# Reordered loads, a held channel product, grouped value products and merged output stores in an attention and mixer kernel

## The chip, the cores and the metric

The kernel runs on one core of one Trainium2 chip. The metric is the device time of one execution in microseconds (us), lower is better. Times are medians of several executions; the profile is one execution, whose span is some 2 us shorter than the time of that same run.

## The reference

Attention with a squared ReLU in place of softmax, its result fed to an MLP mixer (first over tokens, then over channels):

```python
# q, k, v: (8, 12, 448, 64)
scores = q @ k.T / sqrt(64)
attn   = maximum(scores, 0) ** 2 / 448
x      = (attn @ v), heads side by side         # (8, 448, 768)
h = maximum(x.T @ w_tok1, 0) @ w_tok2           # 448 -> 256 -> 448, over tokens
u = x + h.T
out = u + maximum(u @ w_ch1, 0) @ w_ch2         # 768 -> 1536 -> 768, over channels
```

Inputs and output are float32; the kernel computes in bfloat16.

## The kernel before

The work goes in 24 steps of four heads (three steps are one batch). A step transposes q and k on TensorE, makes seven blocks of scores, applies ReLU on ScalarE and squares on VectorE, multiplies by v, transposes the result x back, and does the token products. The channel products of an earlier batch lie in a queue and fill TensorE between them. One unit of the first product is 6 matmuls (about 1.16 us), one of the second 12 (about 1.96 us).

```python
def load_four(i):                       # q, k, v of step i, two transfers each
    ...
        first = i == 0 and name != "v"  # step 0: float32 on SyncE's and ScalarE's queues
        eng = (nc.sync if name == "q" else nc.scalar) if first else nc.gpsimd
        ...
            if first: ...               # and a cast
XDMA = 6                                # up to here x goes back by TensorE, then by DMA
def x_back(i):
    if i >= XDMA:
        for r in range(2):
            nc.sync.dma_start_transpose(out=x_sb[:, r], in_=xT[b % 2][:, 2 * d + r, :])
        return
    ...
def channel2(b, t, half):               # after 12 matmuls and an add into o, [128, 768]
    ...
    if half == 1:
        for k in range(2):              # two stores of 64 rows
            bb, c = divmod(2 * t + k, QC)
            nc.sync.dma_start(
                out=out[2 * (b // 2) + bb].rearrange("(p c) m -> c p m", c=QC)[c],
                in_=o[64 * k : 64 * (k + 1), :],
            )
def channel_work(b):                    # 12 units of the first product, then the second
    ...
# start: loads 0, 1, wt1, 2, wt2, 3, both halves of wc1; then 4, wc2/0, 5, wc2/1, ...
for i in range(DB + 1, ND + 2):         # the steps from 4 on
    scores(i, 0); scores(i, 1)
    values(i - 1, range(5))
    scores(i, 2)
    values(i - 1, range(5, QC)); values_out(i - 1); x_back(i - 1)
    ... fill(1/3) ... scores, transposes(i + 1), token1, token2, fill ...
```

Of the kernel before, what the change touches and what calls it, by code (L numbers as in the profile page):

```python
# [9 lines left out]
FP32 = mybir.dt.float32  # L10
# [6 lines left out]
def kernel(  # L17
# [11 lines left out]
    nc = tc.nc  # L29

    B, H, S, D = q.shape
    DM = H * D
# [5 lines left out]
    DB = H // 4  # L38
    QC = S // 64
    CC = DM // 128  # L40
    EC = DC // 128
# [27 lines left out]


    raws = {}
    first32 = {n: consts.tile([128, 2, QC, D], FP32, name=f"{n}_first") for n in ("q", "k")}

    def load_four(i):
        b, d = divmod(i, DB)
        tiles = []
        for name, src in (("q", q), ("k", k), ("v", v)):
            t = raw.tile([128, 2, QC, D], BF16, name=f"{name}_raw")
            first = i == 0 and name != "v"
            dst = first32[name] if first else t  # L80
            eng = (nc.sync if name == "q" else nc.scalar) if first else nc.gpsimd
            for r in range(2):
                h0 = 4 * d + 2 * r
                eng.dma_start(  # L84
                    out=dst[64 * r : 64 * (r + 1)].rearrange("p g c d -> p g (c d)"),
                    in_=src[b, h0 : h0 + 2].rearrange("g (p c) d -> p g (c d)", c=QC),
                )
            if first:
                if name == "q":
                    nc.vector.tensor_copy(t, dst)  # L90
                else:
                    nc.scalar.copy(t, dst)
            tiles.append(t)
        raws[i] = tiles

# [18 lines left out]
    def load_wc1(i, parts):  # L114
        n = DC // parts
        nc.gpsimd.dma_start(
            out=wc1[:, :, i * n : (i + 1) * n],
            in_=moe_w_ch1.rearrange("(g p) n -> p g n", p=128)[:, :, i * n : (i + 1) * n],
        )
# [11 lines left out]
    def transposes(i, early=False):  # L131
        sb = attn.tile([128, 2, 2, S], BF16, name="qkT")
        if not early:
            both = ps_acc.tile([128, 2, 1024], BF16, tag="acc", name="qkT_ps")
        parts = []
        for w in range(2):
            src = raws[i][w]
            ps = ps_mm.tile([128, 1024], BF16, tag="bank", name="qkT_ps1") if early else both[:, w]
            for c in range(QC):
                for g in range(2):  # L140
                    nc.tensor.matmul(  # L141
                        ps[64 * g : 64 * (g + 1), c * 128 : (c + 1) * 128],
                        lhsT=src[:, g, c, :],
                        rhs=ident,
                        is_transpose=True,
                        start=True,
                        stop=True,
                        skip_group_check=True,
                    )
            parts.append(ps)  # L150
        for w in range(2):
            copy = nc.scalar.copy if early and w == 0 else nc.vector.tensor_copy
            copy(  # L153
                sb[:, :, w, :].rearrange("n r (c p) -> n r c p", c=QC),
                parts[w][:, : 2 * S].rearrange("n (c r p) -> n r c p", c=QC, r=2),
            )
        qkT[i] = sb

    def scores(i, c):
# [54 lines left out]


    x_tiles, r1_tiles, uT_tiles = {}, {}, {}
    XDMA = 6

    def x_back(i):
        b, d = divmod(i, DB)  # L220
        x_sb = mix.tile([128, 2, 4, 128], BF16, name="x_sb")
        x_tiles[i] = x_sb
        if i >= XDMA:
            for r in range(2):
                nc.sync.dma_start_transpose(
                    out=x_sb[:, r], in_=xT[b % 2][:, 2 * d + r, :]
                )
            return
        for r in range(2):
            ps = ps_mm.tile([128, 1024], BF16, tag="bank", name="x_ps")  # L230
            for c in range(4):
                nc.tensor.matmul(
                    ps[:, c * 128 : (c + 1) * 128],
                    lhsT=xT[b % 2][:, 2 * d + r, c * 128 : (c + 1) * 128],
                    rhs=ident,
                    is_transpose=True,
                    start=(c == 0),
                    stop=(c == 3),
                )
            (nc.scalar.copy if r == 0 else nc.vector.tensor_copy)(  # L240
                x_sb[:, r], ps[:, :512].rearrange("n (c d) -> n c d", c=4)
            )

# [76 lines left out]
    def channel2(b, t, half):  # L320
        r2 = r2_tiles[b // 2]
        cols = slice(half * HN, (half + 1) * HN)
        if half == 0:
            out_tiles[b, t] = outp.tile([128, DM], FP32, name="out_sb")
        o = out_tiles[b, t]
        ps = ps_mm.tile([128, 512], FP32, tag="bank", name="m2_ps")
        for e in range(EC):
            nc.tensor.matmul(  # L328
                ps[:, :HN],
                lhsT=r2[:, e, t * 128 : (t + 1) * 128],  # L330
                rhs=wc2[:, e, cols],
                start=(e == 0),
                stop=(e == EC - 1),
            )
        nc.vector.tensor_tensor(  # L335
            out=o[:, cols].rearrange("n (g d) -> n g d", d=128),
            in0=ps[:, :HN].rearrange("n (g d) -> n g d", d=128),
            in1=u_tiles[b][:, half * (CC // 2) : (half + 1) * (CC // 2), t - chunks(b).start, :],
            op=ALU.add,
        )  # L340
        if half == 1:
            for k in range(2):
                bb, c = divmod(2 * t + k, QC)
                nc.sync.dma_start(
                    out=out[2 * (b // 2) + bb].rearrange("(p c) m -> c p m", c=QC)[c],
                    in_=o[64 * k : 64 * (k + 1), :],
                )
            out_tiles.pop((b, t))

    queue = []  # L350
    C1 = 6 * 189
    C2 = 12 * 163

    def channel_work(b):
        u_back(b)
        for e in range(EC):
            queue.append((C1, lambda e=e: channel1(b, e)))
        for t in chunks(b):
            for j in range(2):
                queue.append((C2, lambda t=t, j=j: channel2(b, t, j)))  # L360

    RESERVE = 2500.0
    credit = [-RESERVE]
    per_step = (EC * C1 + NT * C2) / DB

    def fill(share):
        if not queue:
            return
        credit[0] += share * per_step
        while queue and credit[0] > 0:  # L370
            cost, unit = queue.pop(0)
            credit[0] -= cost
            unit()


    PRE = 2
    gate = consts.tile([1, 1], BF16, name="gate")
    warm = consts.tile([128, 512], BF16, name="warm")
    nc.vector.memset(warm, 0.0)
# [12 lines left out]
    load_wt2()  # L392
    load_four(3)
    load_wc1(0, 2)
    load_wc1(1, 2)


    transposes(0, early=True)
    for i in range(DB + 1):
        for c in range(QC):  # L400
            scores(i, c)
            square(keep=1)
            if c < 3 and i > 0:
                values(i - 1, (4 + c,))
                if c == 2:
                    values_out(i - 1)
            if i < DB:
                if c == 3:
                    transposes(i + 1, early=True)
                if c == 4 and i > 0:  # L410
                    x_back(i - 1)
                if c == 5:
                    values(i, (0, 1))
                if c == 6:
                    if i > 0:
                        token1(i - 1)
                    values(i, (2, 3))
                if c == 0 and i > 1:
                    token2(i - 2, early=True)
                if c == 6 and i == 1:  # L420
                    order_wt2()
            else:
                if c == 0:
                    token2(i - 2, early=True)
                if c == 3:
                    x_back(i - 1)
                if c == 4:
                    transposes(i + 1)
                    token1(i - 1)
                if c == 6:  # L430
                    token2(i - 1)
                    channel_work(0)
        if i == 1:
            load_four(4)
            load_wc2(0, 4)
        if i == 2:
            load_four(5)
            load_wc2(1, 4)
    square()
    fill(1 / 3)  # L440

    for i in range(DB + 1, ND + 2):
        if i < ND:
            scores(i, 0)
            scores(i, 1)
        if 0 <= i - 1 < ND:
            values(i - 1, range(5))
        if i < ND:
            scores(i, 2)
        if 0 <= i - 1 < ND:  # L450
            values(i - 1, range(5, QC))
            values_out(i - 1)
            x_back(i - 1)
        if i + PRE < ND:
            if i - 1 >= XDMA:
# [57 lines left out]
```

## Time and profile before

| | before |
|---|---|
| time, median | 403.9 us (403.4 to 404.1) |
| span of the profile | 403.3 us |
| TensorE busy | 380.2 us (94%) |
| TensorE idle, first 100 us | 16.5 us |
| TensorE idle, 100 to 350 us | 1.2 us |
| after the last add | 4.1 us |

The first row is what counts. The prediction below shows and reads the lines behind the others.

### The profile page before, as it was taken

What the parts mean: (1) busy time and instruction counts of PE and PEld (TensorE: products, weight loads), DVE (VectorE), ACT (ScalarE), POOL (GpSimd) and SP (SyncE); (2) the same over time, 40 slices, a digit from 0 to 9 for tenths busy, and PEclk for the clock granted to TensorE, in tenths of its full rate; (3) what the DMA queues carried; (4) which work ended last, traced back from release to release, by engine and by line L of the source; (5) the groups of instructions that cost most, each with busy time, mean ns of one, the idle gap of its engine ahead of it and who ended that gap; (6) DMA issues with size and microseconds to landing.
All of it is one profiled execution on the core that took longest, in us unless ns stands there. A gap on an engine that the chain in (4) does not pass through costs nothing.

```text
span 403.3 us, 8721 instructions
## 1 busy us (share of the span) xinstructions
PE 380.2 (94%) x3609; PEld 205.0 (51%) x3609; DVE 205.5 (51%) x376; ACT 215.9 (54%) x302; POOL 95.8 (24%) x175
## 2 busy tenths in 40 slices
PE   5777888989999999999999999999999999999995
PEld 2344354555545645555445555555445555455563
DVE  1688453465445654565435755456525655452021
ACT  2899367445764456645664456644673456621400
POOL 7952553000123203303033123113033030000000
PEclk9999699999999999999999999999999999999999
DMA  8999999014456596358556496168555592125223
GB/s 172 131 196 202 196 167 167 13 41 106 81 80 119 106 176 91 50 98 164 102 70 121 100 184 98 33 105 153 125 71 88 118 167 61 28 50 117 58 55 102
DMA packets 71880, 43.97 MB, mean 109 GB/s; under 512 B 46048, under 2 KB 68256, under 8 KB 71840
## 3 DMA queue, kind: packets, MB, share of 16 engines
q0 software_dynamic: 24160, 21.24, 37.3%
q1 hardware_dynamic: 47392, 21.71, 25.7%
q10 hardware_dynamic: 288, 0.46, 0.5%
q8 instruction: 28, 0.46, 0.5%
q14 instruction: 12, 0.10, 0.1%
HBM read 43.38 MB, written 11.01 MB: 135 GB/s over the span
## 4 chain that ended last, share of the span: by engine, by line
PE 85%; DMA 7%; DVE 3%; ACT 2%; issue 1%; SPq 1%; POOL 0%; ACTq 0%; DVEq 0%
PE m_ps L328 27%; PE m_ps L311 25%; PE sc_ps L165 10%; PE acc_ps L193 7%; PE t_ps L249 5%; PE qkT_ps L141 5%; PE h_ps L273 5%; DMA k_raw<-in_k_dram 4%; DMA q_first<-in_q_dram 2%; ACT at L174 1%; DVE uT_sb L281 1%; DMA x_sb<-xT 1%; DVE xT L207 1%; DVE at L181 1%; ACT x_sb L240 0%
## 5 line engine op out<-in xcount | busy, mean ns | idle before, releaser
L174 ACT ACTIVATE at<-sc_ps 128x896 bf16<-128x896 f32 x168 | 143.8, 921 | 61.1 <-PE sc_ps L165 61.1
L311 PE MATMUL m_ps<-uT_sb,wc 128*128 128x448 bf16 x576 | 117.6, 353 | 1.3 <-DVE uT_sb L281 0.9
L328 PE MATMUL m_ps<-wc,r_sb 128*128 128x384 bf16 x672 | 116.2, 326 | 0.2 <-ACT x_sb L240 0.2
L181 DVE TENSOR_TENSOR at<-at 128x896 bf16<-128x896 bf16 x168 | 97.1, 617 | 7.9 <-ACT at L174 7.9
L328 PEld LDWEIGHTS <-r_sb 128*128 128x128 bf16 x672 | 64.6, 98 | 44.5 <-issue 2.8
L318 ACT ACTIVATE r_sb<-m_ps 128x448 bf16<-128x448 f32 x96 | 52.2, 544 | 64.2 <-PE m_ps L311 64.2
L311 PEld LDWEIGHTS <-wc 128*128 128x128 bf16 x576 | 54.9, 98 | 55.3 <-issue 8.1
L335 DVE TENSOR_TENSOR out_sb<-m_ps,u_sb 128x384 f32<-128x384 f32 x56 | 31.0, 554 | 56.3 <-PE m_ps L328 56.3
L165 PE MATMUL sc_ps<-qkT 64*64 64x448 bf16 x672 | 53.6, 372 | 3.4 <-ACT at L174 2.5
L207 DVE TENSOR_SCALAR xT<-acc_ps 128x448 bf16<-128x448 f32 x48 | 27.7, 619 | 54.2 <-PE acc_ps L193 54.2
L456 POOL COPY gate<-x_sb 1x1 bf16<-1x1 bf16 x15 | 2.7, 177 | 194.7 <-DMA x_sb<-xT 194.7
L281 DVE TENSOR_TENSOR uT_sb<-h_ps,xT 128x448 bf16<-128x448 f32 x48 | 27.7, 619 | 33.7 <-PE h_ps L273 33.7
L153 DVE COPY qkT<-qkT_ps 128x896 bf16<-128x896 bf16 x44 | 25.6, 619 | 33.1 <-PE qkT_ps L141 33.1
L193 PE MATMUL acc_ps<-at,v_raw 64*64 64x448 bf16 x672 | 42.2, 350 | 0.0
L165 PEld LDWEIGHTS <-qkT 64*64 64x64 bf16 x672 | 17.0, 106 | 36.1 <-issue 31.6
L257 ACT ACTIVATE r_sb<-t_ps 128x512 bf16<-128x512 f32 x24 | 14.4, 600 | 34.0 <-PE t_ps L249 34.0
L84 POOL DMA_DIRECT2D v_raw<-in_v_dram x48 | 29.8, 648 | 8.2 <-PE acc_ps L193 4.4
L84 POOL DMA_DIRECT2D q_raw<-in_q_dram x46 | 27.7, 612 | 16.9 <-DMA wc<-in_moe_w_ch_dram 12.1
L84 POOL DMA_DIRECT2D k_raw<-in_k_dram x46 | 28.0, 631 | 1.4 <-DMA k_raw<-in_k_dram 1.0
L249 PE MATMUL t_ps<-x_sb,wt 128*128 128x256 bf16 x192 | 25.8, 279 | 1.4 <-DMA x_sb<-xT 0.7
L193 PEld LDWEIGHTS <-v_raw 64*64 64x64 bf16 x672 | 20.4, 107 | 10.1 <-issue 1.1
L273 PE MATMUL h_ps<-wt,r_sb 128*128 128x448 bf16 x96 | 23.0, 364 | 0.7 <-ACT wt L109 0.7
(32 smaller groups left out, 116.1 us busy)
## 6 DMA issues: line engine op xcount, KB each, us to landing
out_dram<-out_sb SPq DMA_DIRECT2D x56, 192.0 KB, 2.9
v_raw<-in_v_dram POOLq DMA_DIRECT2D x48, 112.0 KB, 5.1
q_raw<-in_q_dram POOLq DMA_DIRECT2D x46, 112.0 KB, 3.6
k_raw<-in_k_dram POOLq DMA_DIRECT2D x46, 112.0 KB, 4.4
wc<-in_moe_w_ch_dram POOLq DMA_DIRECT2D x2, 1152.0 KB, 13.5
wc<-in_moe_w_ch_dram POOLq DMA_DIRECT2D x4, 576.0 KB, 10.0
u_sb<-uT_sb SPq DMA_TRANSPOSE x48, 3.7
x_sb<-xT SPq DMA_TRANSPOSE x36, 2.4
```

The lines of the kernel that those rows point to most:

```text
L84: eng.dma_start(out=dst[64 * r : 64 * (r + 1)].rearrange("p g c d -> p g (c d)"), in_=src[b, h0 : h0 + 2].rearrange("g (p c) d -> p g (c d ...
L165: nc.tensor.matmul(ps[64 * r : 64 * (r + 1), g, :S], lhsT=sb[h, r, 1, c * 64 : (c + 1) * 64], rhs=sb[h, r, 0, :], start=True, stop=True, s ...
L174: nc.scalar.activation(at, ps[:, :, :S], AF.Relu)
L181: nc.vector.tensor_tensor(out=at, in0=at, in1=at, op=ALU.mult)
L193: nc.tensor.matmul(ps[64 * g : 64 * (g + 1), r, :S], lhsT=v_raw[h, g, c, :], rhs=at[h, g, :], start=(c == 0), stop=(c == QC - 1), skip_gro ...
L207: nc.vector.tensor_scalar(out=xT[b % 2][:, 2 * d + r, :S], in0=ps[:, r, :S], scalar1=float(alpha2), scalar2=None, op0=ALU.mult,)
L249: nc.tensor.matmul(ps[:, j, :], lhsT=wt1[:, c, j * 128 : (j + 1) * 128], rhs=x_sb[:, :, c, :], start=(c == 0), stop=(c == 3),)
L273: nc.tensor.matmul(parts[r][:, :S], lhsT=r1[:, j, r * 128 : (r + 1) * 128], rhs=wt2[:, j, :], start=(j == 0), stop=(j == JC - 1),)
L281: nc.vector.tensor_tensor(out=uT_tiles[b // 2][:, 2 * d + r, off : off + S], in0=parts[r][:, :S], in1=xT[b % 2][:, 2 * d + r, :S], op=ALU.add,
L311: nc.tensor.matmul(ps[:, :S], lhsT=wc1[:, g, e * 128 : (e + 1) * 128], rhs=uT[:, g, off : off + S], start=(g == 0), stop=(g == CC - 1),)
L318: nc.scalar.activation(r2[:, e, off : off + S], ps[:, :S], AF.Relu)
L328: nc.tensor.matmul(ps[:, :HN], lhsT=r2[:, e, t * 128 : (t + 1) * 128], rhs=wc2[:, e, cols], start=(e == 0), stop=(e == EC - 1),)
```

## The change

Its intent is to bring each load when it is needed: the first q and k go first in GpSimd's queue and are cast on the way, the second half of the first channel weight comes after the next q, k, v, and the second channel weight a step later. The second channel product of the first batch is therefore held until the second batch. The value products stand together ahead of the third score block. The output stores change too: where both 64-row groups of a tile belong to one batch, they go out as one store of 2 x 64 rows.

```diff
-    first32 = {...float32 tiles of the first q and k...}
-            first = i == 0 and name != "v"
-            eng = (nc.sync if name == "q" else nc.scalar) if first else nc.gpsimd
-                eng.dma_start(
+                nc.gpsimd.dma_start(
...
-    XDMA = 6
+    XDMA = 7
...                                   # both copies of an x transpose on VectorE
-            (nc.scalar.copy if r == 0 else nc.vector.tensor_copy)(
+            nc.vector.tensor_copy(
...                                   # stores
-            for k in range(2):
-                bb, c = divmod(2 * t + k, QC)
-                nc.sync.dma_start(
-                    out=out[2 * (b // 2) + bb].rearrange("(p c) m -> c p m", c=QC)[c],
-                    in_=o[64 * k : 64 * (k + 1), :],
-                )
+            if b0 == b1:
+                nc.sync.dma_start(out=rows[b0][c0 : c0 + 2, :, part], in_=o[:, part])
+            else:
+                ...                   # two stores of 64 rows, as before
...                                   # the last tile is stored in two halves of its columns
-                queue.append((C2, ...channel2...))
+                later.append((C2, ...channel2...))
+        if b > 0:
+            queue.extend(later); later.clear()
+    rate = [EC * C1 / 3.5]            # back to the full rate from step 7 on
-    PRE = 2
+    PRE = 3
-    load_wc1(1, 2)                    # moved behind load_four(4); wc2 one step later
...
-            values(i - 1, range(5))
+            values(i - 1, range(QC))
+            values_out(i - 1)
             scores(i, 2)
-            values(i - 1, range(5, QC))
-            values_out(i - 1)
```

More of the change, by code (lines that the diff above doesn't have):

```diff
@@ L71 @@
     raws = {}
-    first32 = {n: consts.tile([128, 2, QC, D], FP32, name=f"{n}_first") for n in ("q", "k")}
     def load_four(i):
@@ L78, in load_four @@
             t = raw.tile([128, 2, QC, D], BF16, name=f"{name}_raw")
-            first = i == 0 and name != "v"
-            dst = first32[name] if first else t
-            eng = (nc.sync if name == "q" else nc.scalar) if first else nc.gpsimd
             for r in range(2):
                 h0 = 4 * d + 2 * r
-                eng.dma_start(
-                    out=dst[64 * r : 64 * (r + 1)].rearrange("p g c d -> p g (c d)"),
+                nc.gpsimd.dma_start(
+                    out=t[64 * r : 64 * (r + 1)].rearrange("p g c d -> p g (c d)"),
                     in_=src[b, h0 : h0 + 2].rearrange("g (p c) d -> p g (c d)", c=QC),
                 )
-            if first:
-                if name == "q":
-                    nc.vector.tensor_copy(t, dst)
-                else:
-                    nc.scalar.copy(t, dst)
             tiles.append(t)
@@ L134, in transposes, with copies @@
             both = ps_acc.tile([128, 2, 1024], BF16, tag="acc", name="qkT_ps")
+        def copies(w, ps):
+            halves = [slice(0, 2)] if i > 0 or w == 0 else [slice(0, 1), slice(1, 2)]
+            for n, r in enumerate(halves):
+                on_act = early and (w == 0) == (i > 0) and n == 0
+                (nc.scalar.copy if on_act else nc.vector.tensor_copy)(
+                    sb[:, r, w, :].rearrange("n r (c p) -> n r c p", c=QC),
+                    ps[:, : 2 * S].rearrange("n (c r p) -> n r c p", c=QC, r=2)[:, r],
+                )
         parts = []
@@ L150, in transposes @@
             parts.append(ps)
-        for w in range(2):
-            copy = nc.scalar.copy if early and w == 0 else nc.vector.tensor_copy
-            copy(
-                sb[:, :, w, :].rearrange("n r (c p) -> n r c p", c=QC),
-                parts[w][:, : 2 * S].rearrange("n (c r p) -> n r c p", c=QC, r=2),
-            )
+            if early:
+                copies(w, ps)
+        if not early:
+            for w in range(2):
+                copies(w, parts[w])
         qkT[i] = sb
@@ L340, in channel2 @@
         )
-        if half == 1:
-            for k in range(2):
-                bb, c = divmod(2 * t + k, QC)
-                nc.sync.dma_start(
-                    out=out[2 * (b // 2) + bb].rearrange("(p c) m -> c p m", c=QC)[c],
-                    in_=o[64 * k : 64 * (k + 1), :],
-                )
+        last = b == B - 1 and t == NT - 1
+        if half == 1 or last:
+            part = cols if last else slice(0, DM)
+            (b0, c0), (b1, c1) = divmod(2 * t, QC), divmod(2 * t + 1, QC)
+            rows = [out[2 * (b // 2) + n].rearrange("(p c) m -> c p m", c=QC) for n in range(2)]
+            if b0 == b1:
+                nc.sync.dma_start(
+                    out=rows[b0][c0 : c0 + 2, :, part],
+                    in_=o[:, part],
+                )
+            else:
+                for k, (n, c) in enumerate(((b0, c0), (b1, c1))):
+                    nc.sync.dma_start(
+                        out=rows[n][c, :, part], in_=o[64 * k : 64 * (k + 1), part]
+                    )
+        if half == 1:
             out_tiles.pop((b, t))
-    queue = []
+    queue, later = [], []
     C1 = 6 * 189
@@ L359, in channel_work @@
             for j in range(2):
-                queue.append((C2, lambda t=t, j=j: channel2(b, t, j)))
-    RESERVE = 2500.0
-    credit = [-RESERVE]
-    per_step = (EC * C1 + NT * C2) / DB
+                later.append((C2, lambda t=t, j=j: channel2(b, t, j)))
+        if b > 0:
+            queue.extend(later)
+            later.clear()
+    credit = [0.0]
+    rate = [EC * C1 / 3.5]
     def fill(share):
@@ L368, in fill @@
             return
-        credit[0] += share * per_step
+        credit[0] += share * rate[0]
         while queue and credit[0] > 0:
@@ L434 @@
             load_four(4)
-            load_wc2(0, 4)
+            load_wc1(1, 2)
         if i == 2:
             load_four(5)
+            load_wc2(0, 4)
+        if i == 3:
+            load_four(6)
             load_wc2(1, 4)
     square()
-    fill(1 / 3)
+    fill(1 / 2)
     for i in range(DB + 1, ND + 2):
+        if i == 2 * DB + 1:
+            rate[0] = (EC * C1 + NT * C2) / DB
         if i < ND:
```

## The prediction

> **What bounds the kernel now.** I first read the strip of 40 slices on the page, then a table by windows, because the change acts at the start and the page's averages mix stages.
>
> ```profile
> PE   5777888989999999999999999999999999999995
> PEclk9999699999999999999999999999999999999999
> DMA  8999999014456596358556496168555592125223
> ```
>
> The reader is to see three stages: some 50 us in which TensorE is only 0.5 to 0.8 busy while the DMA engines are full and one slice (40 to 50 us) has a low clock; a long stage in which TensorE is full; and a short end. The window table gives sizes (columns: window, its length, busy us and instruction count of PE, PEld, DVE, ACT, POOL, then granted clock, DMA share, GB/s):
>
> ```profile
> 0.00:10.00 10.00, 5.51 (x37) 2.61 (x37) 1.45 (x5) 2.91 (x4) 7.36 (x18) 1.00 0.90 172
> 10.00:20.00 10.00, 7.77 (x102) 3.90 (x99) 5.96 (x10) 8.42 (x11) 9.74 (x17) 1.00 0.98 131
> 20.00:30.00 10.00, 7.79 (x128) 4.46 (x125) 8.74 (x17) 9.49 (x14) 5.26 (x8) 1.00 1.17 195
> 30.00:40.00 10.00, 7.78 (x118) 4.24 (x114) 8.98 (x18) 9.21 (x14) 2.41 (x4) 1.00 1.21 201
> 40.00:50.00 10.00, 8.00 (x76) 3.95 (x74) 4.50 (x8) 3.94 (x6) 5.62 (x10) 0.66 1.22 195
> ...
> 100.00:350.00 250.00, 248.81 (x2426) 134.16 (x2425) 136.42 (x249) 142.96 (x201) 56.08 (x105) 1.00 0.62 104
> ```
>
> From 100 to 350 us TensorE idles 250 - 248.8 = 1.2 us: nothing is to be had there by reordering, since the change removes no matmul. The idle time is in front: 4.5 us of the first ten, then 2.2, 2.2, 2.2 and 2.0. From 10 to 40 us ScalarE (8.4 to 9.5 of 10) with VectorE right behind it sets the pace, because no channel product exists yet to fill TensorE. Last I read the chain of waits (start, length, what) and TensorE's timeline about the low clock:
>
> ```profile
> 1.56 6.18 DMA q_first<-in_q_dram
> ...
> 7.83 0.64 DVE q_raw L90
> ...
> 24.38 17.64 DMA k_raw<-in_k_dram
> ```
>
> ```profile
> 39.74 0.58 PE L141 MATMUL qkT_ps<-ident,q_raw 128*64 128x128 bf16 x14
> 42.15 0.95 PE L141 MATMUL qkT_ps<-ident,k_raw 128*64 128x128 bf16 x14 [1.82 <-DMA k_raw<-in_k_dram]
> 43.04 1.89 PE L249 MATMUL t_ps<-x_sb,wt 128*128 128x256 bf16 x8
> 44.85 0.96 PE L165 MATMUL sc_ps<-qkT 64*64 64x448 bf16 x8
> 45.75 1.68 PE L273 MATMUL h_ps<-wt,r_sb 128*128 128x448 bf16 x4
> ```
>
> The fifth load of k was issued at 23.8 us and landed near 42 us: it queues behind both 1152 KB halves of the first channel weight (issued at 20.1 and 21.8). TensorE waits 1.82 us, and then runs slow: 14 transposes take 0.95 us against 0.58 just before, and the first token product 1.89 against 1.05 at 24.4 us.
>
> **What the Trainium skill says.** "TensorE: Matmul & The Clock Gate", Part 1 (The HAM clock gate): the array's clock falls to half after about a window of 3.4 us with too little work, and comes back after about as long under load. This trace agrees in kind: the clock is 0.50 from 42 to 46 us and back at 1.00 from 48; here an idle gap of only 1.82 us, after a stage at 0.78 busy, was enough. So a short wait costs more than its length. "DMA: Bandwidth & Descriptors", Anatomy of one DMA — SWDGE: a GpSimd-issued transfer takes about 2.0 us plus its bytes over 436 GB/s; for the 229 KB read by one of the q loads that is an estimate of 2.5 us on an empty queue. The trace's shortest times to landing are 2.9 us (q) and 4.0 us (k), a little more. The same page, "Issuing engines are not separate DMA queues": all queues share the same 16 DMA engines. The trace agrees: the first q and k loads, issued from SyncE and ScalarE within 2.3 us, needed until about 7.8 us, because GpSimd's loads for v and the next group ran beside them (DMA share 1.18 from 4 to 8 us).
>
> **The change, part by part.**
>
> (A) First q and k: they come first in GpSimd's queue, already cast, instead of as float32 over two other queues and a cast. GpSimd starts issuing at 1.43 us and takes 0.61 us for each; the second k transfer is issued from 3.3 to 3.9 us and lands, by the 2.9 to 4.0 us above, at about 6.2 to 7.3. The 14 k transposes (0.45 to 0.9 us) and the copy, now halved between the engines (about 0.55 instead of 0.64), put the first score product at 7.8 to 8.8 us; before it was 10.98. Gain 2.6 us. The other loads of the start are issued some 0.7 us later than before (two transfers more ahead of them on GpSimd, of which 1.9 us of queue waits may vanish), while their use moves 2.6 us forward; the second and third group and the token weights have roughly that much slack. I take nothing off in the middle case.
>
> (B) Steps 0 to 3 are paced by ScalarE. Three copies of x_sb (0.59 us each) go from ScalarE to VectorE, where one costs 0.42. But VectorE is itself busy 8.7 to 9.0 of 10, and the score after each x transpose is held by TensorE's own order (x_ps waited 0.82 us for the ScalarE copy of qkT, which stays). I count 0.2 us a step, 0.6 in all.
>
> (C) Only one half of the first channel weight is now ahead of the fifth q, k, v. The half landed at 31.5 us (GpSimd's queue wait ended then), the other at 37.9, so the k load should land near 34 us, while its transposes are wanted at 39.74 - 2.6 - 0.6 = 36.5. The wait of 1.82 us goes.
>
> (D) With no gap there, the clock should stay. From 42.15 to 48.95 us TensorE spent 6.8 us on k transposes, token products, two score blocks and one channel unit. At later rows' rates the same is 0.42 + 0.87 + 0.50 + 0.77 + 1.16 = 3.7, plus some 0.6 of waits for the ReLU between the token products and for the VectorE add: 4.3. Gain 2.5 us.
>
> (E) Steps 4 to 6 become thin. Before, such a step was 17 us (48.95 to 66.0), about 8 channel units of 1.16 us among 6.75 us of the rest and 0.93 of waits around x_ps (0.73 + 0.20). Now the credit is 12/3.5 = 3.4 units a step, so a step is about 6.75 + 4.0 = 10.75 us of work, and there is less between dependent products. I put the waits at 1.2 us a step instead of 0.93: the third score block now stands behind the values and hides 0.2 of the x_ps wait, but the ReLU between the token products and the squares of the last score blocks are less covered. XDMA = 7 adds one TensorE x transpose: 0.93 us and 0.7 of wait. Loss 3 x 0.3 + 1.6, less what the earlier values_out saves (0.2 x 3): 1.9 us. The held second products (six units of about 1.96 us) aren't lost: the backlog runs later and comes out at the tail, where the kernel before ran its matmuls without gaps (67 in 12.83 us, then 96 in 15.76).
>
> (F) The end. The last add ends at 399.2 us and the span at 403.3; the last output is now two half-width transfers, the first sent 2 us earlier, the second one instruction (0.7 us of issue saved) with half the bytes: 0.8 us. The wait for the last x transpose by DMA (0.53 us at 365.2) is covered by longer fill: 0.5. The other merged output transfers lie beside TensorE and are worth nothing.
>
> Sum: 2.6 + 0.6 + 1.8 + 2.5 - 1.9 + 1.3 = 6.9 us; 403.9 - 6.9 = 397.0.
>
> **The rivals.**
> First, a late load takes the place of the removed one. The DMA engines are saturated until 70 us, so delaying weights only reorders. The sixth q, k, v now follows the second half of the weight: before, its q landed at 47.7 us behind a further 576 KB; without these, at about 0.18 MB/us, it lands near 45 to 46. It is wanted mid step 4, at about 42.5 + 5.5 = 48 us. That is 2 us of slack; if it is late by 1 to 2 us and the clock drops again, 2 to 4 us are given back: 399 to 401. The same could happen to the second and third group at 11 and 18 us, where each 1 us late is simply a smaller A.
> Second, the thin steps become bound by latency, not TensorE. ScalarE needs 7 x 0.82 + 0.6 + 3.4 x 0.5 = 8.0 us and VectorE about 8.4 of a step of 11.9, so neither is the bound, but each in-order wait shows. If a step loses 2 us rather than 1.2, E grows by 2.4: 399.5.
> Third, it goes better: the warm-up matmuls end near 5.2 us; before, TensorE then idled until 8.51 and ran at slow-clock durations until about 17 us. With q landing near 5.5 us it may stay fast, and the VectorE/ScalarE pace may shorten by 0.5 a step: 394 to 395.
> That nothing comes of it (the front being DMA-bound anyway) is contradicted by TensorE's demand: after step 3 it needs attention inputs for only one group in 12 us, 0.69 MB against some 2 MB that the queue delivers.
>
> **Range and chances.** A, C and D have one cause, loads in order of need, and stand or fall together: 5 to 8.5 us. E is -1 to -4.5, F 0.5 to 1.5. I give 393.5 to 400.5 for 8 in 10. Two per cent is 8.1 us, a time below 395.8, which needs the better half of A to D with E small: 0.36. Slower by 2% would need several new late loads: 0.01. Within 2%: 0.63.
>
> **What would show it.** A: the first score row begins at 8 to 9 us. C and D: no wait on k_raw in the fifth transposes and a clock of 0.9 or more from 30 to 50 us; the first channel unit starts near 40 us, before 47.2. E: per step of 4 to 6, three to four channel units and TensorE idle about 1.2 us; idle over 1.5 says I sized it too small, a row waiting on q_raw or k_raw or a clock dip there says the first rival. F: the last output lands about 3.3 us after the last add, before 4.1. From 100 us to the tail, idle must stay near 0.5%; if that stage changes by more than 2 us either way, the order of values and scores matters in a way that I left out.

## The result, and the profile after

The changed kernel takes 473.7 us (471.3 to 475.2, 4 runs) against 403.6 us before (one run more than in the table above). The ratio is 1.173 (1.168 to 1.178). It is 17% slower, far outside the predicted range.

The front did what it should. TensorE's timeline of the changed kernel at the fifth transposes (start, length, instruction, count; a wait would stand in brackets):

```profile
38.01 0.58 PE L140 MATMUL qkT_ps<-ident,q_raw 128*64 128x128 bf16 x14
38.43 0.56 PE L140 MATMUL qkT_ps<-ident,k_raw 128*64 128x128 bf16 x14
38.92 1.05 PE L247 MATMUL t_ps<-x_sb,wt 128*128 128x256 bf16 x8
39.89 0.57 PE L163 MATMUL sc_ps<-qkT 64*64 64x448 bf16 x8
40.71 0.93 PE L271 MATMUL h_ps<-wt,r_sb 128*128 128x448 bf16 x4 [0.25 <-DVE at L179]
```

No wait on k and no slow clock: the same token product that took 1.89 us takes 1.05. The loss is later. The strip of the page of the changed kernel, in 40 slices:

```profile
PE   6888989999775839996799929999499949999930
PEclk8899999999995959999799978999799988999975
```

From the eleventh slice on, about 120 us, TensorE has holes (5, 3, 2, 4, 4 are the deepest) where it was full before, the clock dips at each of these, and the last slice is empty. The waits of the token product on the x that a DMA transpose brings (total us, times, longest), first before, then after:

```profile
PE t_ps L249 <- DMA x_sb<-xT: 0.7, 2, 0.5
```

```profile
PE t_ps L247 <- DMA x_sb<-xT: 49.2, 7, 9.6
```

The chain of waits of the changed kernel shows two of the seven:

```profile
115.72 6.49 DMA x_sb<-xT
122.21 0.05 issue
122.26 1.05 PE t_ps L247 x8
...
161.38 9.98 DMA x_sb<-xT
```

After six of the seven waits (6.2 to 9.6 us each) the token product takes 1.86 to 1.89 us instead of 1.05. After the shortest, of 2.83 us, which is the first one shown here, it takes 1.05.

The table by windows shows the rest (columns as in the prediction). Before, the end:

```profile
350.00:399.20 49.20, 47.90 (x311) 26.51 (x308) 13.40 (x24) 11.61 (x19) 0.00 (x0) 1.00 0.32 73
399.20:403.30 4.10, 0.00 (x0) 0.00 (x0) 0.01 (x1) 0.00 (x0) 0.00 (x0) 0.89 0.38 96
```

After:

```profile
100.00:400.00 300.00, 250.44 (x2335) 134.41 (x2334) 134.89 (x248) 131.31 (x181) 48.89 (x91) 0.91 0.68 84
400.00:450.40 50.40, 49.78 (x290) 28.10 (x288) 8.96 (x16) 10.93 (x20) 0.00 (x0) 1.00 0.23 58
450.40:469.50 19.10, 0.00 (x0) 0.00 (x0) 0.00 (x0) 0.00 (x0) 0.00 (x0) 0.55 0.12 47
```

After the last add nothing computes for 19.1 us, and the stores drain at 47 GB/s with a DMA share of 0.12. Two of sixteen engines are 0.125. That share is the trace's first hint at the cause.

### The profile page after: what moved, and what is told of

It reads as the page before. It is cut to its first block, busy times and chain, and to the rows that moved or that the text cites. A ratio compares the mean times of both kernels' runs of the same rounds, so it can differ in the third digit from the quotient of the medians.

```text
span 469.5 us, 8702 instructions
## 1 busy us (share of the span) xinstructions
PE 386.8 (82%) x3617; PEld 207.6 (44%) x3617; DVE 207.8 (44%) x384; ACT 211.8 (45%) x295; POOL 98.2 (21%) x177
## 4 chain that ended last, share of the span: by engine, by line
PE 72%; DMA 13%; SPq 4%; DVE 4%; ACT 3%; issue 1%; POOL 1%; ACTq 0%; POOLq 0%
PE m_ps L309 24%; PE m_ps L326 21%; DMA x_sb<-xT 12%; PE sc_ps L163 7%; PE acc_ps L191 6%; PE t_ps L247 6%; PE h_ps L271 4%; PE qkT_ps L140 3%; SPq L297 3%; ACT at L172 2%; DVE xT L205 2%; DVE at L179 1%; DMA k_raw<-in_k_dram 1%; PE x_ps L230 1%; ACT r_sb L255 1%
## 5 line engine op out<-in xcount | busy, mean ns | idle before, releaser
L309 PE MATMUL m_ps<-uT_sb,wc 128*128 128x448 bf16 x576 | 122.4, 363 | 0.5 <-DVE uT_sb L279 0.5
L309 PEld LDWEIGHTS <-wc 128*128 128x128 bf16 x576 | 56.8, 101 | 55.3 <-issue 9.2
L247 PE MATMUL t_ps<-x_sb,wt 128*128 128x256 bf16 x192 | 30.0, 308 | 49.3 <-DMA x_sb<-xT 49.2
L247 PEld LDWEIGHTS <-wt 128*128 128x128 bf16 x192 | 19.7, 108 | 58.5 <-DMA x_sb<-xT 43.1
L129 DVE COPY qkT<-qkT_ps 128x896 bf16<-128x896 bf16 (+1 forms) x45 | 26.0, 615 | 32.3 <-PE qkT_ps L140 29.9
L191 PE MATMUL acc_ps<-at,v_raw 64*64 64x448 bf16 x672 | 38.5, 352 | 0.0
L79 POOL DMA_DIRECT2D q_raw<-in_q_dram x48 | 29.0, 612 | 29.1 <-DMA wc<-in_moe_w_ch_dram 22.8
L79 POOL DMA_DIRECT2D k_raw<-in_k_dram x48 | 29.1, 623 | 1.3 <-DMA q_raw<-in_q_dram 0.8
L163 PEld LDWEIGHTS <-qkT 64*64 64x64 bf16 x672 | 15.0, 106 | 31.6 <-issue 27.8
```

Source lines behind the costliest of these rows:

```text
L79: nc.gpsimd.dma_start(out=t[64 * r : 64 * (r + 1)].rearrange("p g c d -> p g (c d)"), in_=src[b, h0 : h0 + 2].rearrange("g (p c) d -> p g ...
L163: nc.tensor.matmul(ps[64 * r : 64 * (r + 1), g, :S], lhsT=sb[h, r, 1, c * 64 : (c + 1) * 64], rhs=sb[h, r, 0, :], start=True, stop=True, s ...
L191: nc.tensor.matmul(ps[64 * g : 64 * (g + 1), r, :S], lhsT=v_raw[h, g, c, :], rhs=at[h, g, :], start=(c == 0), stop=(c == QC - 1), skip_gro ...
L247: nc.tensor.matmul(ps[:, j, :], lhsT=wt1[:, c, j * 128 : (j + 1) * 128], rhs=x_sb[:, :, c, :], start=(c == 0), stop=(c == 3),)
L309: nc.tensor.matmul(ps[:, :S], lhsT=wc1[:, g, e * 128 : (e + 1) * 128], rhs=uT[:, g, off : off + S], start=(g == 0), stop=(g == CC - 1),)
```

## The experiments

Three theories stood at first. Theory 1: a merged store, whose slowest dimension is 2, runs on two of the 16 DMA engines, and the x transposes wait for those two. Theory 2: the held products, the thin steps or the deeper prefetch cost the time. Theory 3: stores of 384 KB are slow in themselves, or hold SyncE's sequencer. Each run is compared with the kernel before in the same rounds. The diffs are shortened.

**e1_unmerged**: the changed kernel with 64-row stores.

```diff
-            if b0 == b1:
+            if False:
```

> The changed kernel with one thing undone: each output tile goes out as two 64-row stores again, none as one store of 2 x 64 rows. Theory 1 (the merged stores run on 2 of the 16 DMA engines, and the x transposes of the same queue wait behind them): nearly all of the 70 us go away, and what is left is the gain of the front of the kernel; by its trace, which reaches step 8 about 9 us ahead of the kernel before at equal work, 393 to 398 us, and no wait of the token product on x_sb above 1 us. Theory 2 (the held second products, the thin steps or the deeper prefetch cause the loss): it stays above 450 us.

Measured 395.66 us (395.39 to 397.12), ratio 0.980 (0.976 to 0.985): faster than the kernel before, though whether by 2% is unclear. This one edit takes away 78 us, and theory 2 falls. Its windows:

```profile
100.00:340.00 240.00, 238.97 (x2340) 130.66 (x2338) 135.41 (x249) 131.48 (x182) 49.27 (x91) 1.00 0.63 105
...
389.90:393.80 3.90, 0.00 (x0) 0.00 (x0) 0.02 (x1) 0.00 (x0) 0.00 (x0) 0.86 0.31 69
```

The two profiles add up. The spans differ by 469.5 - 393.8 = 75.7 us. The token product's waits are 49.2 us against none on x here, the drain after the last add 19.1 against 3.9 (15.2), and TensorE's busy time 386.8 against 375.4 for the same matmuls (11.4), because after six of the seven waits it runs at the slow clock for a while. 49.2 + 15.2 + 11.4 = 75.8.

**e2_before_merged**: the kernel before with only the merged stores.

```diff
+            if b0 == b1:
+                nc.sync.dma_start(out=rows[b0][c0 : c0 + 2], in_=o)
```

> The kernel before with only the merged stores of 2 x 64 rows added. Theory 1: the whole loss appears without any other part of the change, 460 to 485 us, with some 20 us of stores after the last add (23 MB/s-like figures aside: DMA share near 2/16 = 0.13 in that tail). Theory 2: within 3 us of 403.6.

Measured 513.29 us, ratio 1.270 (1.264 to 1.277). The merged stores alone make the loss, and a larger one than expected: 109 us here, 78 in the changed kernel. Most of the difference stands in the waits: the token products wait 74.4 us on x here, in ten waits, against 49.2 in seven. I did not test why. In the changed kernel five units of the second product more (14 against 9) come after the last token product, where their stores delay no x transpose; that would work in this direction.

**e3_store_actq**: the changed kernel with the merged stores on ScalarE's queue.

```diff
             if b0 == b1:
-                nc.sync.dma_start(
+                nc.scalar.dma_start(
```

> The changed kernel with the merged stores issued from ScalarE's queue instead of SyncE's, still 2 x 64 rows. Theory 1 in its strict form (x transposes wait because they stand in the same rings behind slow stores): the waits of the token products mostly go, the slow drain after the last add stays, 405 to 425 us. If the stores slow down whatever shares the two engines, not only their own queue, it stays above 440. Theory 3 (SyncE's sequencer held by long issues is the cause, not the rings): also 405 to 425, and no slow drain at the end.

Measured 474.75 us, ratio 1.176: no change. So it isn't the place behind the stores in one queue, nor SyncE's sequencer; the strict form of theory 1 and that part of theory 3 fall. (In the changed kernel 4% of the chain that ended last is SyncE's queue issuing; here it is 0%, the share of the x transposes grows from 12% to 17%, and the time is the same.) But this run shows the engine count, because now the stores have a queue to themselves on the page (packets, MB, share). In the kernel before that queue, q10, held only two 64-row loads of the first k; here it holds 25 stores:

```profile
q10 hardware_dynamic: 288, 0.46, 0.5%
```

```profile
q10 hardware_dynamic: 3250, 9.44, 5.3%
```

The two loads are 2 x 128 runs of data, 256 packets; the remaining 32 are 16 completion packets for each. The 25 stores have 25 x 128 rows, 3200 packets; the remaining 50 are two for each. A 64-row transfer finishes on 16 engines, a 2 x 64 store on two.

**e4_rows62_2, e6_rows48_16, e7_rows57_7**: the kernel before with each 64-row store cut in two, so that nothing is merged and only the row count differs.

```diff
+                for p0, p1 in ((0, 62), (62, 64)):          # or 48, or 57
+                    nc.sync.dma_start(out=rows[p0:p1], in_=o[64 * k + p0 : 64 * k + p1, :])
```

> The kernel before with every 64-row store cut into 62 and 2 rows: four smaller stores in place of two, none of them merged. If the number of engines is the largest number up to 16 that divides the first dimension, both pieces get 2 engines. Theory 1: as slow as the merged stores, 455 to 490 us. Theory 3 (a store of 384 KB or of two row groups is what is slow): at most a few us over 403.6 for the doubled issues.

> The kernel before with every 64-row store cut into 48 and 16 rows: the same number of stores as in the 62 and 2 run, and both pieces divisible by 16. If the engine count is the largest divisor up to 16 of the row count, all 16 engines work and the time stays within 3 us of 403.6, against 530 us with 62 and 2. If small or many stores were the cause there, it is above 450 us here too.

> The same with 57 and 7 rows: by the divisor rule 3 engines (57 = 3 x 19) and 7. Each of the three then carries 19 rows of a store where the two carried 31, so the loss of 127 us of the 62 and 2 run should shrink by more than the ratio 19/31: 430 to 480 us. If uneven row counts cost by themselves (not their divisors), it is near 530 us as with 62 and 2.

Measured 530.35 us (ratio 1.313), 407.78 us (1.010) and 450.41 us (1.117). The waits of the token product on x, in the order 62 and 2, 57 and 7, 48 and 16:

```profile
PE t_ps L249 <- DMA x_sb<-xT: 88.0, 12, 9.8
```

```profile
PE t_ps L249 <- DMA x_sb<-xT: 29.4, 10, 5.6
```

```profile
PE t_ps L249 <- DMA x_sb<-xT: 3.7, 6, 1.5
```

All three issue the same number of stores and move the same bytes, in pieces smaller than before. The largest divisors up to 16 of the row counts differ: 2 and 2, 3 and 7, 16 and 16. The loss goes 126, 47, 5 us. Size and number of the stores are not the cause. The 5 us of the last were more than the 3 expected; I put them down to the doubled number of stores.

The page of each run counts the engines of the stores themselves, which I had overlooked. SyncE's queue (packets, MB, share), before, then in the same order:

```profile
q1 hardware_dynamic: 47392, 21.71, 25.7%
q1 hardware_dynamic: 46720, 21.70, 39.1%
q1 hardware_dynamic: 47056, 21.71, 36.0%
q1 hardware_dynamic: 48288, 21.71, 26.6%
```

The rows are the same, so only completion packets can differ. For each of the 56 stores cut in two they change by -12, -6 and +16. With 16 for a whole store, the two pieces have 4, 10 and 32 together: 2 + 2, 3 + 7 and 16 + 16. In the same way e2 has 720 packets less than before, 30 for each of its 24 merged stores: 2 in place of 32.
The Trainium skill says this outright ("DMA: Bandwidth & Descriptors", Why a DMA increments its semaphore by 16 and not by 1): the number of engines of a transfer is the largest number up to 16 that divides the size of the slowest dimension on both sides. Every run here agrees: share 0.12 and two completions for 2 x 64 rows, 16 completions for 64.

**e5_store_pool**: the changed kernel with the merged stores on GpSimd's queue.

```diff
-                nc.sync.dma_start(
+                nc.gpsimd.dma_start(
```

> The changed kernel with the merged stores (still 2 x 64 rows, 384 KB) issued from GpSimd's queue. Moving them to ScalarE's queue changed nothing (474.8 against 473.7 us), so what counts is not the queue but the two DMA engines that every merged store and every x transpose share. The Trainium skill has GpSimd's transfers start on another engine each time, or on all 16. If the same two engines are loaded every time is what hurts: below 430 us. If a 384 KB store in two row groups is slow in itself, or any store late in the step hurts: above 450 us. A loss of up to some 20 us may come from loads waiting behind stores in GpSimd's queue.

Measured 460.17 us, ratio 1.140: a miss. I had reasoned that spreading the stores over changing engines would do. The profile (KB each, us from issue to landing) shows why the idea was weak:

```profile
out_dram<-out_sb POOLq DMA_DIRECT2D x23, 384.0 KB, 12.5
...
x_sb<-xT SPq DMA_TRANSPOSE x34, 4.8
```

The store itself still takes 12.5 us against 2.9 for half as much before, and x takes 4.8 us against 2.4. If a transfer over all 16 engines has to wait for its slowest one, it does not matter which engines a slow store holds; that is argued, not shown. What the expectation says of GpSimd's transfers stands in "DMA: Bandwidth & Descriptors", Why a DMA increments its semaphore by 16 and not by 1. Which engines these stores ran on the trace does not tell, so whether they rotate stays open.

**e11_merged_xpe and e12_unmerged_xpe**: the changed kernel with merged and with 64-row stores, and all x transposes on TensorE.

```diff
-    XDMA = 7
+    XDMA = 24
```

> The changed kernel with its merged stores, but with all x transposes on TensorE (XDMA = 24), so that no token product waits for a DMA transpose any more; the same with 64-row stores runs beside it. If the merged stores hurt only by delaying the DMA transposes of x, the 78 us between the two kinds of store shrink to the slow drain at the end: this run is 10 to 25 us over its 64-row twin, near 425 to 445 us. If they hold TensorE in another way (output buffers, loads of q, k, v, u transposes), the distance stays above 50 us.

> The changed kernel with 64-row stores and all x transposes on TensorE: 17 more of them at 0.93 us of TensorE and some 0.5 to 0.7 us of wait for the scaling on VectorE: 395.7 + 17 x 1.5 = 421 us, 412 to 428. It is the twin of the run before and no theory of the stores touches it.

Measured 438.61 and 421.27 us, ratios 1.087 and 1.042; both as expected. Without DMA transposes of x on the path, the 78 us between the two kinds of store shrink to 17. The windows after the last add, merged, then not:

```profile
417.60:437.10 19.50, 0.00 (x0) 0.00 (x0) 0.00 (x0) 0.00 (x0) 0.00 (x0) 0.54 0.12 46
```

```profile
414.10:418.50 4.40, 0.00 (x0) 0.00 (x0) 0.00 (x0) 0.00 (x0) 0.00 (x0) 0.70 0.26 60
```

19.5 - 4.4 = 15.1 us of the 18.6 between the spans is the slow drain. So most of the loss comes in two ways: the merged stores delay the DMA transposes that TensorE waits for (and the clock falls in those waits), and they end the kernel late.

**e8_not_held**: e1 with the second product of the first batch not held (queue, rate and reserve of before).

```diff
-                later.append((C2, ...))
+                queue.append((C2, ...))
...
-    credit = [0.0]
-    rate = [EC * C1 / 3.5]
+    credit = [-2500.0]
+    rate = [(EC * C1 + NT * C2) / DB]
...
-    fill(1 / 2)
+    fill(1 / 3)
```

> The changed kernel with 64-row stores (395.7 us) and the second channel product of the first batch not held: the queue, rate and reserve of the kernel before, with the new order of loads. The second channel weight lands last near 83 us, and the kernel before used it from 75 us on. If holding is what makes the new load order safe, TensorE waits on the second weight at 65 to 85 us and the time is 398 to 405 us. If holding is worth nothing, within 1 us of 395.7.

Measured 400.11 us, ratio 0.992 (0.988 to 0.996), against 0.980 for e1 (in other rounds, so I compare the ratios to the kernel before); the intervals don't meet. Holding, with the rate that goes with it, is worth about 1.2%. TensorE now waits for the late weight, though for less than I had thought:

```profile
PE m_ps L326 <- DMA wc<-in_moe_w_ch_dram: 1.5, 1, 1.5
```

This wait is 1.5 of some 4.7 us. Most of the rest stands in the same table: three waits of the token product on x by DMA, 3.2 us in all, where e1 has none.

**e9_split_values**: e1 with the value products split around the third score block.

```diff
-            values(i - 1, range(QC)); values_out(i - 1)
+            values(i - 1, range(5))
             scores(i, 2)
+            values(i - 1, range(5, QC)); values_out(i - 1)
```

> The changed kernel with 64-row stores and the value products split again around the third score block, as in the kernel before. By the prediction the new order hides 0.2 us of the wait for the x transpose in each of four steps and is worth nothing in the steps that fill TensorE: 396 to 397.5 us against 395.7.

Measured 399.08 us, ratio 0.988 (0.984 to 0.991). That is some 3 us over e1 where I expected 1; the intervals of the two ratios just touch, so the sign is likely and the size is rough. The timelines show a cause in the full stage. The kernel before, which has the old order too, then e1:

```profile
208.49 1.12 PE L193 MATMUL acc_ps<-at,v_raw 64*64 64x448 bf16 x20
209.60 0.38 PE L165 MATMUL sc_ps<-qkT 64*64 64x448 bf16 x4
209.78 0.57 PE L193 MATMUL acc_ps<-at,v_raw 64*64 64x448 bf16 x8
210.29 1.31 PE L311 MATMUL m_ps<-uT_sb,wc 128*128 128x448 bf16 x6
```

```profile
202.64 1.49 PE L191 MATMUL acc_ps<-at,v_raw 64*64 64x448 bf16 x28
203.96 0.36 PE L163 MATMUL sc_ps<-qkT 64*64 64x448 bf16 x4
204.26 3.58 PE L309 MATMUL m_ps<-uT_sb,wc 128*128 128x448 bf16 x18
```

The same 32 matmuls occupy TensorE for 210.29 - 208.49 = 1.80 us in the old order and 204.26 - 202.64 = 1.62 in the new. Neither order shows a wait here; it is busy time that shrinks. The step shown is one of the better ones: in e9 the 32 matmuls occupy 1.69 to 1.88 us, in e1 1.61 to 1.68. Over the run TensorE is busy 378.0 us in e9 and 375.4 in e1, which is 2.6 us of the 3.9 between the spans. The rest is in waits, chiefly on the x that a DMA brings (1.1 us against none) and of x transposes on VectorE (3.8 against 3.0).

**e13_fill_first**: e1, and in steps 4 to 7 the channel unit stands before the x transpose on TensorE instead of behind it.

```diff
+        if i - 1 < XDMA:
+            fill(1 / 3)
         x_back(i - 1)
         ...
-        fill(1 / 3)
+        if not i - 1 < XDMA:
+            fill(1 / 3)
```

> An attempt at a better kernel: the changed kernel with 64-row stores, and in the four thin steps the channel unit that stood after the x transpose on TensorE stands before it, so that it covers the wait for VectorE (0.55 us a step in the trace) and for the copy. 393 to 395 us against 395.7; no gain if VectorE's copies only move the wait behind the transpose.

Measured 393.49 us (392.98 to 395.74), ratio 0.975 (0.971 to 0.978): clearly faster than before, and the best kernel here. Its interval overlaps that of e1 by a little, so its lead of about 2 us over e1 is likely, not certain. Of the 3.0 us in which x transposes waited for VectorE in e1, 0.8 remain, and a new wait for ScalarE stands in part of their place:

```profile
PE x_ps L230 <- ACT r_sb L316: 1.6, 4, 0.4
```

## Why the prediction was wrong

The step that failed is one sentence of (F): "The other merged output transfers lie beside TensorE and are worth nothing." They cost 78 us. I took the number of transfers and their bytes as their cost, and did not ask on how many engines each one runs, though the order of dimensions was in the diff and the rule on a page that I had open. And I took "beside TensorE" as settled from the stores' own place, though x transposes on the path use the same engines. The prediction even quoted that all queues share the engines. Among the rivals, which dealt with late loads, thin steps and the warm-up, none had this. Neither the first nor the third came: up to 100 us TensorE waits on no q or k after the first k, and the transposes at 12.20 us took 0.96 us, as slow as those before.

The other steps, read from the timelines of before and after:

- (A) and (B), predicted 2.6 and 0.6 us. The first score row began at 8.86 us instead of 10.98, 2.1. The fifth transposes began at 38.01 instead of 39.74, 1.7. So A was a little smaller (the transposes of the first k waited until 7.66 us, past the 6.2 to 7.3 at which it was to land), and B was worth nothing: the copies taken from ScalarE bought no pace.
- (C), 1.8 us: right. The wait on k is gone.
- (D), 2.5 us: measured 1.9. From the start of the fifth q transposes to the first score row of step 4, before took 48.95 - 39.74 = 9.2 us and after 44.66 - 38.01 = 6.65, in which it did one channel unit more (1.16); the difference is 3.7, of which C is 1.8. The clock was 1.00 from 30 to 50 us.
- (E), a loss of 1.9: measured about nothing. From the value products of step 4 to those of step 8, before takes 67.2 us with 22 first and 6 second units, after 51.7 with 19 first units. Less 1.16 and 1.96 us a unit, they leave 29.9 and 29.7 us. The extra x transpose was paid for by shorter waits (0.55 us at each x transpose instead of 0.73 + 0.20) and the grouped values (1.68 us instead of 1.87).
- (A) to (E) together: predicted 5.6, measured 1.7 + 1.8 + 1.9 + 0.2 = 5.6 us by the start of step 8, with A, B and D too large and E too pessimistic. This agreement is luck: the errors cancel, and in e1's profile the fifth transposes begin 0.5 us later (38.53 us) with the same code up to there.
- (F), the end: with 64-row stores, 3.9 us after the last add against 4.1, where I had said 3.3. The wait at the last x transpose is gone as predicted.
- Left out: the order of the value products in the full stage. I wrote that nothing was to be had there by reordering, because there is no idle time. The grouped order shortens busy time by some 0.1 to 0.2 us a step. The first sign that I named (idle near 0.5%) could not see it; the second, a stage that changes by more than 2 us, was the right one.

Without the stores, the kernel is at 395.7 us against the predicted 397.0. That closeness is partly luck too: e9, without the gain that I had left out, took 399.1. That the rest of the change was read nearly right does not save the prediction: the line that I dismissed was more than ten times the sum of the others.

## What to carry to other kernels

Before merging transfers, look at the slowest dimension of both sides: make it a multiple of 16, or leave the transfers apart. A store over two engines was slow here, and it held up transfers beside it: in e5 an x transpose landed after 4.8 us instead of 2.4, and in the changed kernel a q load after 6.1 us instead of 4.5 in e1. Check stores as if they were on the path whenever anything on the path goes by DMA. And a stage without idle time can still shrink, as it did here when the value products stood together; count busy time a step, not only waits.

## What the Trainium skill lacked or had wrong

- "DMA: Bandwidth & Descriptors", Why a DMA increments its semaphore by 16 and not by 1: the rule on the number of engines is right, and the page repeats it in its rules for kernel authors, but its price isn't given. Here it was 78 us on top of 396 for 25 merged stores, and 126 us for stores of 62 and 2 rows in place of 64.
- The same page, Issuing engines are not separate DMA queues: right, but it does not say that a transfer on few engines holds up those on other queues. Moving the slow stores to ScalarE's queue left 474.8 us against 473.7, and on GpSimd's queue it was still 460.2.
- The same page, Anatomy of one DMA — SWDGE: its formula gives 2.5 us for one early load; in the first 85 us of the kernel before, the q loads landed after 2.9 us at best, 6.5 in the median and 16.1 at worst. Not wrong, but no guide to a busy start.
- "TensorE: Matmul & The Clock Gate", Part 1: it gives an idle window of about 3.4 us, and says that frequent short gaps can do the same, without a length. In the kernel before a gap of 1.82 us, after a stage at 0.78 busy, was followed by 4 us at half clock; in the changed kernel a gap of 2.83 us, after a full stage, was not.
- I found no page with the price of alternating small matmul blocks: 0.1 to 0.2 us a step for 20 + 4 + 8 against 28 + 4 matmuls of 64 x 64.
